# Attention and two MoE layers on one core: values' products of two tiles together, values' sums later, attention a step further ahead

## The chip, the cores and the metric

One core of a Trainium2 chip runs the whole program. The metric is the device time in microseconds (us). The engines are TensorE (PE in the profile, with its weight loads as PEld), VectorE (DVE), ScalarE (ACT), GpSimd (POOL) and SyncE (SP), which here only issues DMAs. Each takes its own instructions in their written order and waits at semaphores for the others.

## The reference

Three layers follow one another. The attention has 4 batches, 8 heads, 576 positions and 64 columns a head; a cumulated bias and a causal mask are added to the scores. Its output is laid out as 2304 tokens of 512 columns. Two feed-forward layers (called MoE) of 2048 inner columns follow, one with a squared ReLU, one with h cos h.

```python
scores = scale * np.matmul(q, k.transpose(0, 1, 3, 2))
cum = np.cumsum(np.maximum(s, 0.0), axis=-1)
bias = -(cum[:, :, :, None] - cum[:, :, None, :])
scores = np.where(causal, -1000000000.0, scores + np.minimum(bias, 0.0))
attn = softmax(scores)                 # with 1e-09 added to the sum
x = np.matmul(attn, v)                 # to 2304 x 512
h = np.maximum(x @ w_in, 0.0);  x = h * h @ w_out
h = x @ w_in2;                  out = (h * np.cos(h)) @ w_out2
```

## The kernel before

The 2304 tokens are cut into nine blocks of 256. Attention produces a block's tokens as a *unit*: eight heads, and in each head tiles of up to 128 queries (128 or 64). There are 160 such tiles, called jobs and numbered in order; the first 32 (heads below `EARLY`, 256 positions) take a short path in f32, the other 128 the path that this text is about. The first MoE layer then works block by block in 16 *chunks* of 128 inner columns: `g1` (line 844, 12 products of 256 columns), then two chunks later `g2` (line 873, 12 products). Every operand is split into a high and a low part, so each product comes three times. The second layer (lines 1230 and 1285) follows from about 620 us on.

Attention is laid between the chunks by hand. `step()` advances the job number i by one and emits, in this order: `g1` or `g2` of one chunk, the evacuation of finished heads on DVE (`evacuate`, ending at line 630), the mask and row minimum of job i-1 (line 510) and the split of job i-2 into two f16 parts `p` (lines 555 and 559) with its transposing DMA on SP (line 565, `p` to `pt`), the low part `gl` of earlier chunks (line 863), the scores of job i on PE (line 496), further chunks, the exponentials on ACT, then the products with the values on PE (`emit_pv`, line 590: 9 to 15 products for a wide tile, 3 or 6 for a narrow one), and the transposes of evacuated heads on PE (`turn`, line 644). `LAG` says how many steps after its scores a job's products with the values come: 3 for the early jobs, 5 for the others. `unit_done` says at which step block u's chunks begin: the lag of its last job and 3 more.

At the end of a block's chunks the two halves of its result leave PSUM: `yst` is copied on ACT (first half) and on DVE (second half), line 881, stored by SP, and squared and summed on ACT (line 884). The next block's first `g2` reuses the same PSUM.

The values themselves are split beside all this: `v_load`, `v_square` (ACT, line 390), `v_sum` (a tiny product on PE over the squares' sums, line 398), `v_scale`, `v_high`, `v_low`, `v_store`. `V_TIME` is the number of steps that `v_steps` reserves for it, `v_add` puts each on its step.

Buffers that matter: `p` has two of 1280 columns, and a third under the tag `p3` for every third job once the first layer's weights are split; `pt` has three; `stg` has two of 2 KB a partition, for weights under way and for `yst`; `pvs`, in which the products with the values gather, has two halves for successive pairs of heads. A tile that finds its pool full is written only when the last user of the buffer it gets has finished.

Of the kernel before, what the change touches and what calls it, by code (L numbers as in the profile page):

```python
# [10 lines left out]
F16 = mybir.dt.float16  # L11
# [12 lines left out]
NF = DFF // 128  # L24
# [9 lines left out]
LAG = (3, 5)  # L34
# [62 lines left out]
EARLY = 16  # L97
# [10 lines left out]
XST_TO = 20  # L108
V_STRIDE = 11
V_NEAR = 6  # L110
V_TIME = 7


@with_exitstack
def attention_moe_moe_kernel(
# [24 lines left out]
    wp = ctx.enter_context(tc.tile_pool(name="wp", bufs=1))  # L140
# [4 lines left out]
    at = at_stack.enter_context(tc.tile_pool(name="at", bufs=1, side="right"))  # L145
# [48 lines left out]
    for x in range(H // 2):  # L194
        t = wp.tile([128, 2, 2 * BT], F32, tag=f"w{2 * NF - (2, 3, 4, 6)[x]}", name="early")
# [113 lines left out]
    for x in range((XST + 1) // 2):  # L309
        t = wp.tile([128, 2, 512], F32, tag=f"w{2 * NF - 5 - x}", name="xst")  # L310
# [6 lines left out]
    jobs = []  # L317
    last_job = {}
# [8 lines left out]
    jd = {}  # L327
    xb = {}
    evq, xtq, xcq = [], [], []
    lag1, wrest = [], []  # L330
# [117 lines left out]
    def v_steps(gs, start):  # L448

        at, due = [], len(jobs) + V_TIME  # L450
        for b, h, n, nch in reversed(gs):
            first = next(
                i for i, j in enumerate(jobs) if j[0] >= 2 * H and heads[j[0]][1] == b and h <= heads[j[0]][2] < h + n
            )
            due = min(first - start + 3 - V_TIME, due - V_NEAR)
            at.insert(0, due)
# [6 lines left out]
    def v_add(gs, at, stored=True):  # L463

        for g, t in zip(gs, at):
            fs = []
            if g not in vs:
                fs, t = [(t, v_load)], t + 2
            fs += [(t, v_square), (t + 1, v_sum), (t + 2, v_scale), (t + 2, v_high), (t + 3, v_low)]
            for x, f in fs + [(t + 3, v_store)] * stored:  # L470
                vq.extend([] for _ in range(x + 1 - len(vq)))
                vq[x].append((f, g))

# [42 lines left out]
        j["sb"], j["nb"] = sb, nb[0:r, len(j["ps"]) - 1:len(j["ps"])]  # L516

    def p_tile(i):
        third = nw[2] >= 2 * NF and not wrest and i % 3 == 2
        return at.tile([128, 1280], F16, tag="p3" if third else "p", bufs=1 if third else 2, name="p")  # L520

    def emit_exp(i):
# [17 lines left out]
    def emit_split(i):  # L540
        n, ti, q, r = jobs[i]
        j = jd[i]
        w, sb = j["w"], j["sb"]
        cw = 128 * ((w + 127) // 128)
        if n < EARLY:
            pp = j["ps"][0][0][:, BT:BT + cw]
            pt = at.tile([128, 640], F32, tag="pt", bufs=3, name="pt1")
            (nc.scalar.copy if ti else nc.vector.tensor_copy)(pt[:, 0:w], pp)
            j["pt"] = pt
            yield  # L550
            return
        p = p_tile(i)
        if cw > w:
            nc.gpsimd.memset(p[0:r, 0:2 * cw].rearrange("p (a c) -> p a c", a=2)[:, :, w:cw], 0.0)
        nc.vector.tensor_scalar(
            out=p[0:r, 0:w], in0=sb[0:r, 0:w], scalar1=PSC, scalar2=None, op0=ALU.mult
        )
        yield
        nc.vector.scalar_tensor_tensor(  # L559
            out=p[0:r, cw:cw + w], in0=sb[0:r, 0:w], scalar=PSC, in1=p[0:r, 0:w],  # L560
            op0=ALU.mult, op1=ALU.subtract,
        )
        pt = at.tile([128, 1280], F16, tag="pt", bufs=3, name="pt")
        pt = pt[:, 0:2 * cw // 128 * r].rearrange("p (a r) -> p a r", r=r)
        nc.sync.dma_start_transpose(out=pt, in_=p[0:r, 0:2 * cw])
        j["pt"] = pt
        yield
# [106 lines left out]
    def job(i):  # L674
        return jobs[i] if 0 <= i < NJ else None

    def lag(i):
        return LAG[not job(i) or jobs[i][0] >= EARLY]

    def heads_ahead(i, *fs):  # L680
        if job(i) and jobs[i][1] == 0:
# [1 line left out]
                upto(cnt, jobs[i][0] + d, f)  # L683

    def unit_done(u):
        return last_job[u] + lag(last_job[u]) + 3


    nw = [2, 0, 0]
    stq = [(wp, 3)]  # L690
    p3 = [0]
# [285 lines left out]
    def softmax_tail(i):  # L977
        if job(i - 1):
            yield from emit_mask(i - 1)
        for j in stage(2, i - 2):  # L980
            yield from emit_split(j)

    def step(moe=0, bits=0, attn=True):
# [37 lines left out]
        if attn:  # L1021
            for j in stage(0, i - 2):
                if jobs[j][1] == 0:
                    load_v(jobs[j][0])
            for j in stage(3, i - LAG[0]):
                if j > i - lag(j):
                    stages[3] -= 1
                    break
                emit_pv(j)
# [104 lines left out]
    while prog[0] < unit_done(0):  # L1134
        i = prog[0]
        x = i - FIRST_BITS
        step(bits=int((x + 1) * PROLOG_BITS) - int(x * PROLOG_BITS) if x >= 0 else 0)

    for k in range(NB1):
        start = prog[0]  # L1140
        goal = unit_done(k + 1) if k + 1 < NB1 else start
        if k == 0:
            gs = [(b, h, 2, 5) for b in V_ORDER for h in range(0, H, 2)]
            v_add(gs, v_steps(gs, start))
# [164 lines left out]
    for i in range(len(steps2) + G2LAG):  # L1309
# [6 lines left out]
        if new:  # L1316
            p, j, f = steps2[i]
# [89 lines left out]
```

## Time and profile before

| | |
|---|---|
| median of 3 runs | 1003.15 us (1000.76 to 1003.25) |
| the profiled execution | 1003.76 us, of which 1002.0 us are its span |
| PE busy | 966.9 us (96%) |
| DVE busy | 723.9 us (72%) |
| ACT busy | 655.5 us (65%) |
| POOL busy | 163.2 us (16%) |
| mean granted clock of PE | 0.995 |

Attention's late jobs lie between about 107 and 560 us. In the rows below, a row of the timeline gives the start in us, the duration in us, engine, line, operation and tiles; xN says that N like instructions in a row are merged into it; a bracket at its end says how long the engine sat idle before it and for what. Successive matmuls overlap, so what a product costs PE is the distance from its start to the next start.

### The profile page before, as it was taken

What the parts mean: (1) busy time and instruction counts of PE and PEld (TensorE: products, weight loads), DVE (VectorE), ACT (ScalarE), POOL (GpSimd) and SP (SyncE); (2) the same over time, 40 slices, a digit from 0 to 9 for tenths busy, and PEclk for the clock granted to TensorE, in tenths of its full rate; (3) what the DMA queues carried; (4) which work ended last, traced back from release to release, by engine and by line L of the source; (5) the groups of instructions that cost most, each with busy time, mean ns of one, the idle gap of its engine ahead of it and who ended that gap; (6) DMA issues with size and microseconds to landing.
All of it is one profiled execution on the core that took longest, in us unless ns stands there. A gap on an engine that the chain in (4) does not pass through costs nothing.

```text
span 1002.0 us, 20487 instructions
## 1 busy us (share of the span) xinstructions
PE 966.9 (96%) x7266; PEld 740.6 (74%) x7266; DVE 723.9 (72%) x1865; ACT 655.5 (65%) x1596; POOL 163.2 (16%) x258
## 2 busy tenths in 40 slices
PE   5999899999999999999999999999999999999998
PEld 4788898899999998999999997444544454444444
DVE  6879788867777897787888267798887545555555
ACT  4789777767777777767776578777766444433433
POOL 2000011111111121111211023330033341000000
PEclk9999999999999999999999999999999999999999
DMA  8955599746887986467898569210000000011001
GB/s 268 292 182 181 118 202 203 170 111 157 196 162 160 178 193 175 109 155 145 192 206 180 188 237 360 95 43 1 1 1 1 0 1 1 0 43 43 23 20 64
DMA packets 150711, 126.65 MB, mean 126 GB/s; under 512 B 108048, under 2 KB 125792, under 8 KB 150608
## 3 DMA queue, kind: packets, MB, share of 16 engines
q1 hardware_dynamic: 146688, 119.05, 46.1%
q0 software_dynamic: 3904, 6.29, 2.5%
q8 instruction: 57, 0.93, 0.4%
q14 instruction: 46, 0.38, 0.1%
q10 hardware_dynamic: 16, 0.01, 0.0%
HBM read 85.25 MB, written 15.81 MB: 101 GB/s over the span
## 4 chain that ended last, share of the span: by engine, by line
PE 79%; DVE 8%; DMA 6%; ACT 4%; issue 2%; SPq 1%; DVEq 0%; ACTq 0%
PE hps L844 18%; PE y L873 18%; PE o L1285 17%; PE hp L1230 17%; PE qkp L496 4%; PE pvs L590 4%; DMA rw<-in_w_dram 3%; DMA raw<-in_qk_dram 1%; PE xps L644 1%; DVE st L716 1%; DVE sb L510 1%; DVE gl L863 1%; DVE wt L737 0%; DVE k L357 0%; SPq L178 0%
## 5 line engine op out<-in xcount | busy, mean ns | idle before, releaser
L844 PE MATMUL hps<-xh,wt 128*128 128x256 f32 x1152 | 241.4, 292 | 4.1 <-ACT g L855 4.0
L873 PE MATMUL y<-gh,wt 128*128 128x256 f32 x1152 | 237.7, 289 | 0.0
L844 PEld LDWEIGHTS hps<-xh,wt 128*128 128x128 f32 x1152 | 191.7, 194 | 7.0 <-ACT g L855 5.5
L873 PEld LDWEIGHTS y<-gh,wt 128*128 128x128 f32 x1152 | 189.9, 192 | 1.3
L1230 PE MATMUL hp<-yh,wt 128*128 128x512 f16 (+1 forms) x640 | 185.9, 358 | 0.0
L1285 PE MATMUL o<-wt,gh 128*128 128x512 f16 x576 | 171.3, 379 | 2.0 <-ACT wt L1300 1.9
L873 PE MATMUL y<-gl,wt 128*128 128x256 f32 x576 | 163.4, 284 | 2.6 <-DVE gl L863 2.6
L844 PE MATMUL hps<-xl,wt 128*128 128x256 f32 x576 | 164.3, 285 | 0.9 <-DVE xl L661 0.9
L1230 PEld LDWEIGHTS <-wt 128*128 128x128 f16 x960 | 92.2, 98 | 93.3
L1242 ACT ACTIVATE a<-hp,hsc 128x512 f32<-128x512 f32 (+1 forms) x80 | 51.4, 643 | 118.6 <-PE hp L1230 117.2
L855 ACT ACTIVATE g<-hps 128x256 f32<-128x256 f32 x144 | 54.6, 379 | 107.7 <-PE hps L844 105.8
L1230 PE MATMUL hp<-yl,wt 128*128 128x512 f16 (+1 forms) x320 | 114.4, 358 | 0.0
L873 PEld LDWEIGHTS y<-gl,wt 128*128 128x128 f32 x576 | 110.6, 192 | 3.7 <-DVE gl L863 3.1
L844 PEld LDWEIGHTS hps<-xl,wt 128*128 128x128 f32 x576 | 111.7, 194 | 1.4 <-DVE xl L661 1.1
L1285 PE MATMUL o<-wt,gl 128*128 128x512 f16 x288 | 109.2, 379 | 0.4 <-DVE gl L1272 0.4
L1243 DVE TENSOR_SCALAR kf<-a 128x512 f32<-128x512 f32 (+1 forms) x80 | 34.5, 431 | 103.8 <-ACT a L1242 103.4
L1285 PEld LDWEIGHTS <-gh 128*128 128x128 f16 x576 | 56.2, 98 | 66.7 <-issue 2.4
L527 ACT ACTIVATE sb<-sb,nb 128x128 f32<-128x128 f32 (+8 forms) x160 | 93.7, 586 | 12.1 <-DVE nb L510 12.0
L339 POOL DMA_DIRECT2D k<-ext_d x80 | 40.8, 510 | 341.9 <-ACT g L856 92.3
L510 DVE CUSTOM_DVE_ANT_0 sb<-qkp,mask 128x128 f32<-128x128 f32 (+8 forms) x160 | 72.7, 454 | 13.8 <-PE qkp L487 8.6
L1251 ACT ACTIVATE a<-kf 128x512 f32<-128x512 f32 (+1 forms) x80 | 46.8, 585 | 46.6 <-DVE kf L1244 46.1
L559 DVE SCALAR_TENSOR_TENSOR p<-sb,p 128x512 f16<-128x512 f32 (+7 forms) x128 | 72.4, 565 | 4.0
(119 smaller groups left out, 1680.1 us busy)
## 6 DMA issues: line engine op xcount, KB each, us to landing
rw<-in_w_dram SPq DMA_DIRECT2D x64, 512.0 KB
raw<-in_qk_dram SPq DMA_DIRECT2D x32, 352.0 KB
raw<-in_qk_dram SPq DMA_DIRECT2D x16, 384.0 KB
v_d<-vt SPq DMA_DIRECT2D x16, 320.0 KB
raw<-in_qk_dram SPq DMA_DIRECT2D x16, 320.0 KB
vb<-v_d SPq DMA_DIRECT2D x32, 160.0 KB
vr<-in_v_dram POOLq DMA_DIRECT2D x15, 320.0 KB, 4.7
y_d<-yst SPq DMA_DIRECT2D x18, 256.0 KB
```

The source lines that it names most:

```text
L339: nc.gpsimd.dma_start(out=hd[n][1][64:68, BT - nq:BT + nl], in_=ext_d[n, :, BT - nq:BT + nl])
L496: nc.tensor.matmul(p[0:r, 0:cn], m[0:kk, qo:qo + r], m[0:kk, BT + c0:BT + c0 + cn], start=(kk == 128), stop=(kk == 68),)
L510: nc.vector.tensor_tensor_reduce(out=sb[0:r, c0:c0 + cn], in0=p[0:r, 0:cn], in1=mask[0:r, mo + c0:mo + c0 + cn], scale=-0.125, scalar=(3.0 ...
L527: nc.scalar.activation(out=sb[0:r, 0:w], in_=sb[0:r, 0:w], func=ACTF.Exp, scale=-1.0, bias=j["nb"], accum_out=pd[n - h % 2]["z"][0:r, ti, ...
L559: nc.vector.scalar_tensor_tensor(out=p[0:r, cw:cw + w], in0=sb[0:r, 0:w], scalar=PSC, in1=p[0:r, 0:w], op0=ALU.mult, op1=ALU.subtract,)
L844: nc.tensor.matmul(hp, w[:, a, c * 128:(c + 1) * 128], (xh, xl)[e][:, c, :], start=(n == 0), stop=(n == 3 * KD - 1),)
L855: nc.scalar.activation(out=g, in_=hp, func=ACTF.Relu)
L873: nc.tensor.matmul(yps[k][d // 2][:, d % 2, :], w[:, a, d * 128:(d + 1) * 128], (gh, gl)[e], start=(f == 0 and n == 0 and d % 2 == 0), sto ...
L1230: nc.tensor.matmul(hp, w[:, a, c * 128:(c + 1) * 128], (yh, yl)[e][:, c, :], start=(m == 0), stop=(m == 3 * KD - 1),)
L1242: nc.scalar.activation(out=a, in_=hp, func=ACTF.Copy, scale=sm["hsc"][:, j, f:f + 1], bias=0.25)
L1251: nc.scalar.activation(out=a, in_=kf, func=ACTF.Sin, scale=-6.2831850)
L1285: nc.tensor.matmul(ops[j][a], (gh, gl)[e][:, a * 128:(a + 1) * 128], w[:, x, :], start=(first and m == 0), stop=(last and m == 2),)
```

## The change

Six edits. The lag of a late job becomes 5 for an even and 4 for an odd number, so that jobs i and i+1 have their products with the values in the same step. `unit_done` adds 4 instead of 3 from the second unit on. The values' sum, scales, high and low parts and store come one step later behind the squares, and `V_TIME` reserves 8 steps. The third `p` buffer serves only jobs of up to 512 positions. Of `pt`, jobs whose number leaves 3 by 4 take other memory: the `p3` buffer where the tile is wider than 512 positions, one of the two `stg` buffers otherwise. The arithmetic is the same.

```diff
-V_TIME = 7
+V_TIME = 8
...
-            fs += [(t, v_square), (t + 1, v_sum), (t + 2, v_scale), (t + 2, v_high), (t + 3, v_low)]
-            for x, f in fs + [(t + 3, v_store)] * stored:
+            fs += [(t, v_square), (t + 2, v_sum), (t + 3, v_scale), (t + 3, v_high), (t + 4, v_low)]
+            for x, f in fs + [(t + 4, v_store)] * stored:
...
-        third = nw[2] >= 2 * NF and not wrest and i % 3 == 2
+        third = nw[2] >= 2 * NF and not wrest and i % 3 == 2 and jd[i]["w"] <= 512
...
-        pt = at.tile([128, 1280], F16, tag="pt", bufs=3, name="pt")
+        if i % 4 < 3:
+            pt = at.tile([128, 1280], F16, tag="pt", bufs=3, name="pt")
+        elif cw > 512:
+            pt = at.tile([128, 1280], F16, tag="p3", bufs=1, name="pt3")
+        else:
+            pt = wp.tile([128, 1024], F16, tag="stg", bufs=2, name="pt4")
...
-        return LAG[not job(i) or jobs[i][0] >= EARLY]
+        if job(i) and jobs[i][0] < EARLY:
+            return LAG[0]
+        return LAG[1] - (i % 2 if job(i) else 0)
...
-        return last_job[u] + lag(last_job[u]) + 3
+        return last_job[u] + lag(last_job[u]) + (4 if u else 3)
```

Line numbers in the changed kernel are higher by 5 (values' products 595, turns 649) or 7 (chunks 851 and 880, copies of `yst` 888).

On PE, before, in the second half of the fourth unit: a wide tile's products with the values (`pvs` from `pt`), two turns (`xps` from `xp`), a values' sum, then a chunk, and the narrow tile of the same head a chunk later.

```order
L844 MATMUL hps_77<-xh_1815,wt_695 128x256
L590 LDWEIGHTS pt_3126
L590 MATMUL pvs_78<-vb_3154,pt_3126 128x64
...
L644 MATMUL xps_79<-ident_85,xp_3259 128x128
L644 MATMUL xps_79<-ident_85,xp_3259 128x64
L398 MATMUL xps_79<-ss_3241,ones_87 128x2
L873 MATMUL y0_2909<-gh_3149,wt_539 128x256
...
L496 MATMUL qkp_3337<-k2_3197 128x256
L590 LDWEIGHTS pt_3185
L590 MATMUL pvs_78<-vb_3154,pt_3185 64x64
```

On PE, after, at the same place: the two tiles of the head stand together.

```order
L851 MATMUL hps_77<-xh_1749,wt_695 128x256
L595 LDWEIGHTS pt_3135
L595 MATMUL pvs_78<-vb_3162,pt_3135 128x64
...
L595 LDWEIGHTS pt_3185
L595 MATMUL pvs_78<-vb_3162,pt_3185 64x64
...
L398 MATMUL xps_79<-ss_3202,ones_87 128x2
L880 MATMUL y0_2932<-gh_3157,wt_539 128x256
```

Over the program the 128 groups of products with the values become 64, all of two tiles: 40 pairs of two 128-row tiles, 8 of two 64-row tiles, 16 of one of each. Of the 48 places with turns, 36 stand right behind such a group before, and none after, because `turn` now falls in the steps between.

On DVE, before, at the end of the first block's chunks (`y1` is the second half of the block's result; the names in brackets are the semaphores that the instruction waits for, DMAHW being DMAs):

```order
L404 TENSOR_SCALAR vsc_89<-xps_79 128x2 [waits PE_49]
L555 TENSOR_SCALAR p_1540<-sb_1466 128x512 [waits Activation_49]
L409 TENSOR_SCALAR vsc_89<-vsc_89 128x2 [waits DVE_49]
L559 SCALAR_TENSOR_TENSOR p_1540<-sb_1466,p_1540 128x512 [waits DVE_49]
L881 COPY yst_1571<-y1_646 128x512 [waits PE_49]
L510 ISA sb_1607,nb_1608<-qkp_1551,mask_86 128x512 [waits DVE_49]
```

On DVE, after, at the same place:

```order
L559 SCALAR_TENSOR_TENSOR p_1583<-sb_1490,p_1583 128x384 [waits DVE_49]
L354 TENSOR_TENSOR hi_1563<-raw_1363,hi_1563 64x256 [waits DMAHW4_49,Activation_49]
L357 TENSOR_TENSOR k2_1564<-raw_1363,hi_1563 64x512 [waits DMASW5_49]
L888 COPY yst_1615<-y1_646 128x512 [waits DMAHW5_49,PE_49,Activation_49]
L425 SCALAR_TENSOR_TENSOR vt_1418<-vr_1314,vsc_89,vt_1418 128x5x64 [waits DMAHW1_49,DMASW4_49]
```

Here one `stg` buffer holds job 35's `pt`, so both halves of `yst` get the other one: the copy of `y1` waits for the store and the squaring of the first half. At the eight later block ends both `stg` buffers are free again.

On DVE, before, in the fourth unit, where its narrow heads begin (job 56's `p`, in the third `p` buffer):

```order
L510 ISA sb_2890,nb_2891<-qkp_2850,mask_86 64x192 [waits DVE_49,PE_49]
L510 ISA nb_2891 64x1
L555 TENSOR_SCALAR p_2893<-sb_2839 128x128 [waits DMAHW3_49,Activation_49,Pool_49]
L559 SCALAR_TENSOR_TENSOR p_2893<-sb_2839,p_2893 128x128 [waits DVE_49]
L661 TENSOR_TENSOR xl_2673<-xps_79,xh_2672 128x64 [waits Activation_49]
```

On DVE, after, the same job:

```order
L510 ISA sb_2914,nb_2915<-qkp_2853,mask_86 64x192
L510 ISA nb_2915 64x1
L555 TENSOR_SCALAR p_2917<-sb_2841 128x128 [waits DMAHW4_49,PE_49,Activation_49]
L559 SCALAR_TENSOR_TENSOR p_2917<-sb_2841,p_2917 128x128 [waits DVE_49]
L354 TENSOR_TENSOR hi_2893<-raw_2766,hi_2893 64x192 [waits DMAHW6_49,Activation_49]
```

Its buffer last held job 55's `pt`, so it now waits for PE: for job 55's products with the values, which stand a step later than this write. The same happens once more, at job 113 behind job 111.

## Rows read from the trace of the kernel before

**Rows 1.** Busy time by stretch: us and instructions of each engine, clock, DMA share, GB/s
```profile
105.00:117.50 12.50, 9.94 (x77) 9.24 (x76) 11.27 (x30) 9.51 (x25) 1.29 (x2) 1.00 0.75 169
...
300.00:350.00 50.00, 50.00 (x496) 48.68 (x495) 39.21 (x104) 38.33 (x103) 6.10 (x11) 1.00 0.83 170
...
505.00:520.00 15.00, 15.00 (x157) 14.83 (x156) 13.71 (x41) 12.13 (x31) 2.15 (x6) 1.00 0.81 191
```

**Rows 2.** Timeline of PE: waits in the attention stretch
```profile
109.97 0.44 PE L644 MATMUL xps<-ident,xp 128*128 128x128 f32 x2 [0.38 <-DVE xp L630]
...
114.25 0.39 PE L844 MATMUL hps<-xl,wt 128*128 128x256 f32 x1 [0.88 <-DVE xl L661]
...
117.74 0.38 PE L398 MATMUL xps<-ss,ones 128*128 128x2 f32 x2 [1.55 <-ACT vt L390]
...
195.55 0.63 PE L590 MATMUL pvs<-vb,pt 128*64 128x64 f16 x15 [1.39 <-DVE xp L630]
...
387.27 0.63 PE L590 MATMUL pvs<-vb,pt 128*64 128x64 f16 x15 [1.11 <-DVE xp L630]
...
523.34 0.39 PE L844 MATMUL hps<-xh,wt 128*128 128x256 f32 x1 [1.40 <-ACT g L855]
```

**Rows 3.** Busy time by stretch, right behind two of these waits
```profile
117.50:122.50 5.00, 4.76 (x25) 4.57 (x26) 1.22 (x4) 1.50 (x6) 0.37 (x1) 0.66 0.17 58
...
195.00:200.00 5.00, 4.45 (x34) 4.34 (x34) 4.03 (x16) 3.08 (x10) 0.55 (x2) 0.66 1.38 311
```

**Rows 4.** Timeline of PE: a wide tile's nine products between two chunks
```profile
301.78 0.28 PE L844 MATMUL hps<-xh,wt 128*128 128x256 f32 x1
301.90 0.43 PE L590 MATMUL pvs<-vb,pt 128*128 128x64 f16 x9
302.17 0.36 PE L873 MATMUL y<-gh,wt 128*128 128x256 f32 x1
302.38 0.28 PE L873 MATMUL y<-gl,wt 128*128 128x256 f32 x1
```

**Rows 5.** Timeline of PE: a 64-row tile's fifteen products behind the scores
```profile
396.23 0.28 PE L496 MATMUL qkp<-k 68*128 68x256 f32 x1
396.44 0.66 PE L590 MATMUL pvs<-vb,pt 128*64 128x64 f16 x15
...
397.25 0.28 PE L844 MATMUL hps<-xl,wt 128*128 128x256 f32 x1
```

**Rows 6.** Timeline of PE: a turn alone, and a turn behind fifteen products
```profile
505.88 0.33 PE L644 MATMUL xps<-ident,xp 128*128 128x128 f32 x1
...
506.17 0.28 PE L844 MATMUL hps<-xl,wt 128*128 128x256 f32 x1
...
517.34 0.61 PE L590 MATMUL pvs<-vb,pt 128*128 128x64 f16 x15
...
518.05 0.28 PE L844 MATMUL hps<-xl,wt 128*128 128x256 f32 x1
```

**Rows 7.** Waits of SP's queue: us in total, times, longest
```profile
SPq L565 <- PE pvs L590: 81.5, 71, 3.9
```

**Rows 8.** Timeline: the two copies at the end of the first block
```profile
122.39 0.59 ACT L881 COPY yst<-y 128x512 f32<-128x512 f32 x1 [0.31 <-PE y L873]
...
123.11 0.69 DVE L881 COPY yst<-y 128x512 f32<-128x512 f32 x1 [3.72 <-PE y L873]
```

**Rows 9.** DMA issues of the page: KB each, median us from issue to landing
```profile
vr<-in_v_dram POOLq DMA_DIRECT2D x15, 320.0 KB, 4.7
...
k<-ext_d POOLq DMA_DIRECT2D x32, 11.0 KB, 3.3
```

**Rows 10.** Timeline of the last unit: writes of p, one transposing DMA, its landing
```profile
529.18 0.46 DVE L555 TENSOR_SCALAR p<-sb 128x576 f16<-128x576 f32 x1
...
531.67 1.32 SPq L565 DMA_TRANSPOSE pt<-p  x1
...
535.16 0.20 POOL L554 MEMSET p<- 128x128 f16 x1 [0.23 <-DMA pt<-p]
...
537.24 0.46 DVE L555 TENSOR_SCALAR p<-sb 128x576 f16<-128x576 f32 x1
```

## The prediction

> **What bounds the kernel now.** I read the busy times first, by engine and then by stretch. PE is at 96% of the span, and in the middle of the attention it has no gap at all: 50.00 of 50 us, while DVE has 39 and ACT 38 [rows 1]. There a microsecond less on PE is a microsecond less of the program, and nothing else helps. In the stretch before it, while the first layer's weights are still being split, DVE is the tight one (11.27 of 12.5 us, PE 9.94), and in the last unit both are (13.71 and 15.00 of 15) [rows 1]. Then I went along PE's timeline for its waits. Six matter here [rows 2]: at 109.97 a turn and at 114.25 the first chunk of the second block wait for DVE, which is just finishing the unit before; at 117.74 the values' sum waits 1.55 for squares that ACT made a step earlier; at 195.55 and 387.27 the products with the values wait 1.39 and 1.11 for DVE to empty the accumulator, both times right after a block's end, where DVE also had a copy to do; at 523.34 a chunk waits 1.40 for ACT, which stood waiting for a load. Behind two of them the granted clock is 0.66 over 5 us [rows 3]: part of that stretch at the lower of the two levels, 1.7 us of clock lost each (0.34 x 5). Last I looked at what PE pays between two chunks.
>
> **The switch between kinds of products.** Consecutive products of a chunk start 0.12 apart (301.78 to 301.90). From 301.78 to 302.38, two such starts, it is 0.60; nine products with the values took 0.27 of it (301.90 to 302.17, 0.03 each), so 0.60 - 0.24 - 0.27 = 0.09 is the price of leaving the chunk and coming back, paid in the first product behind (0.21 in place of 0.12) [rows 4]. For a 64-row tile it is more: 396.23 to 397.25 is 1.02; less 0.24, and less 15 products at about 0.033 (0.66 less one product's 0.19 latency, over 14 steps; estimate) makes 0.28 [rows 5]. With 128 groups made into 64, 40 pairs save 0.09 each (3.6), 8 pairs of 64-row tiles 0.28 each (2.3), and 16 mixed pairs 0.09 each if the narrow half still pays all of its 0.28 (1.4): 7.3 us together. What a mixed join costs no row shows: between nothing (then it saves up to 0.28 a pair) and a whole narrow switch more, 7.3 lies between about 3 and 10; I take the middle one, since the narrow switch is measured.
>
> Against that stand the turns. Behind a group they ride on its switch: 517.34 to 518.05 is 0.71, less 0.45 for 15 products, 0.12 for one chunk product due and 0.09 for the switch, so a single turn costs 0.05. Alone, with its start 0.12 behind the product before it, 0.12 + 0.29 - 0.24 = 0.17 [rows 6]. So each of the 36 places that lose their group costs 0.12 more, 4.3 us. The values' sums (16) lose theirs about half the time, under 1 us, and I leave them in the range. **First term: -7.3 + 4.3 = -3.0 us** (-6 to +1).
>
> The Trainium skill (TensorE: Matmul & The Clock Gate, "Step-by-step: what each phase is for") speaks against this term: the next tile's weights are loaded while the present tile's matmul runs, so a change of tile should cost no time. Inside one kind of product the trace agrees (0.12 each, with loads beside them). At the change of kind it does not, and by rows 4 the first product behind is 0.09 late. By the page the term would be 0 and the whole sum 3.0 higher; the measurement decides.
>
> **Values' sums later, attention ahead.** The sum's wait at 117.74 goes, because a full step lies between squares and sum. With the unit finished one step before its block begins, the waits at 109.97 and 114.25 go too. Together 0.38 + 0.88 + 1.55 = 2.8 us, and with the clock behind the last one (1.7) 4.5. But DVE is at nine tenths there [rows 1] and all the work remains, with one attention step more put ahead of the second block; part of what PE no longer waits for here it waits for a little later. **Second term: -2.5 us** (-4.5 to +1).
>
> **Accumulator emptied in time.** A pair of heads' last products and the next pair's first were a step apart, with DVE's emptying of `pvs` between. Now two steps lie between, as products come every second step only. The waits of 1.39 and 1.11 go, with 1.7 of clock at most: 4.2. At both places DVE is late for what follows as well (its copies of `yst` have just been made), so I take half. **Third term: -2.0 us** (-4.2 to 0).
>
> **SP's queue.** With three `pt` buffers each transposing DMA waited for the products with the values of three jobs earlier: 81.5 us over 71 waits [rows 7], and loads of raw heads stood behind it on SP. With a fourth place for `pt` this wait is gone. Almost all of it hid; where it showed is 523.34, ACT waiting for such a load. I take half of those 1.40. **Fourth term: -0.7 us** (-2.8 to 0).
>
> **The copy of y1.** At the first block's end DVE's copy now waits for the store of the other half, and ACT's squaring of it waits for DVE. From the moment `y0` is complete: 0.59 for ACT's copy [rows 8], a store of 256 KB that no row shows, bounded by the page's loads at 3.3 (11 KB) and 4.7 (320 KB) [rows 9], 0.69 for DVE's copy: 4.6 to 6.0. In that time PE has the other half of the chunk, a chunk, the scores and half of the next block's first `g2`: 24 products of 0.12 and two long ones at about 0.24 (twice a 256-column product, estimate), 3.3. Left over: 1.3 to 2.7; with lost clock up to 4.4; nothing if PE is late there anyway; a gain is excluded, as nothing is taken away. **Fifth term: +2.0 us** (0 to +4.4).
>
> The Trainium skill (DMA: Bandwidth & Descriptors, "Anatomy of one DMA") puts a DMA at about 2.0 us fixed, most of it the receipt of a write, and bytes over 436e3; that is an estimate of 2.6 us for this store. By it the copy would be ready after 3.9 us, PE would wait 0.6, and the sum would be 1.4 lower. No row here shows a store's landing.
>
> **Edits that I cost at nothing.** At jobs 56 and 113 DVE waits at the write of `p` for PE. What is queued behind it on DVE is the next head's low parts and the next chunks' `gl`; PE has one chunk (1.4 us) ahead of the next scores and about four us of work ahead of the `gl` concerned, and DVE has room there. Uncovered it would be about 1 us each, inside the range. Two `p` buffers where a tile is wider than 512: the transposing DMA landed at 535.16, 6.0 after its write of `p` began at 529.18, and the next but one write begins at 537.24 [rows 10], so 2.1 us are left, and SP's wait inside the 6.0 goes. The step that the unit is ahead changes no count: late units had lag 5 + 3 behind an odd last job, and have 4 + 4.
>
> **Sum.** -3.0 - 2.5 - 2.0 - 0.7 + 2.0 = -6.2 us against the profiled execution's 1003.76 us: 997.6. The execution lay 0.6 above the median of the runs shown; I forecast 997.5 us, 0.56% below it. What a measurement of this kernel can tell from no change is about 0.3%, 3 us: faster is below 1000.1, slower above 1006.2.
>
> **Rivals.**
> *DVE takes it back.* The waits removed were all on DVE or ACT, and these have as much to do as before. If PE only meets them at the next place, terms two to four come to nothing and the copy of `y1` stays: 1003.8 - 3.0 + 2.0 = 1002.8. For it: DVE at 90% around 110 us and in the last unit. Against it: from 300 to 350 it is at 78%, and DVE itself waited 3.72 for PE at 123.11 [rows 8]. No change.
> *All of it stays.* Terms two to four in full and the copy hidden: 1003.8 - 3.0 - 4.5 - 4.2 - 2.8 = 989.3.
> *Two p buffers bind (slower).* In the last unit and in the first halves of the fourth and the seventh, 32 steps, a write of `p` may have to wait for the transposing DMA of two jobs earlier. It decides from a landing 2.1 us later than in rows 10; 0.8 us beyond that costs 0.4 a step, 32 x 0.4 = 12.8 less what the other terms gain (6.2): 1010. For it: the queues are full there and the buffer that goes was used. Against it: the DMA now starts earlier.
> *No switch saved.* By the page's rule the first term is 0, and with the others 1000.6: no change.
>
> **How the numbers follow.** The forecast has a chance of 0.47 (its own range 993 to 1000), all of it stays 0.14, DVE takes it back 0.25, two p buffers 0.10, no switch saved 0.04. Of the forecast's share nearly all is faster: 0.47 + 0.14 = 0.61. Within 0.3%: 0.25 + 0.04 = 0.29. Slower: 0.10. The range of 8 in 10 leaves out the slower rival and half of the largest gain: 990.5 to 1004.0.
>
> **What would show it.** Products with the values on PE in 64 groups, each switch still 0.09 or 0.28, turns alone at 0.17; no wait at the values' sums and none of PE for DVE's emptying behind a block's end; SP's wait for products with the values nearly gone; one wait of PE of one to three us at the first `g2` of the second block, with DVE and ACT idle before it. The prediction is wrong if busy PE between 200 and 500 us does not get shorter by about 2 us, if PE's waits between 100 and 200 us add up to as much as before, or if DVE waits for transposing DMAs in the wide units.

## The result, and the profile after

Forecast: 997.5 us. Measured: 1007.92 us, the median of 8 runs (1004.71 to 1011.15), against 1001.68 us for the kernel before in the same runs (1000.62 to 1003.25). The ratio is 1.0058, interval 1.0039 to 1.0078: slower by about 6 us, outside the range (990.5 to 1004.0). The profiled execution took 1007.96 us. The profiled execution of before, on which the sum was made, lay with 1003.76 us above all eight of these runs.

The page after, span and busy times:

```profile
span 1006.2 us, 20471 instructions
PE 964.5 (96%) x7266; PEld 741.5 (74%) x7266; DVE 721.1 (72%) x1865; ACT 654.6 (65%) x1596; POOL 162.6 (16%) x258
```

PE is busy for 2.4 us less than before, and the span is 4.2 us longer. The stretches after, first two disturbed ones and then an undisturbed one (columns as in [rows 1]):

```profile
80.00:100.00 20.00, 16.67 (x112) 16.10 (x111) 16.10 (x43) 16.34 (x44) 1.06 (x3) 0.83 0.60 206
205.00:215.00 10.00, 6.89 (x57) 6.35 (x58) 7.06 (x31) 4.02 (x12) 0.52 (x2) 0.83 0.31 79
276.48:350.83 74.35, 74.35 (x751) 73.06 (x749) 56.19 (x155) 56.67 (x153) 8.47 (x19) 1.00 0.84 172
```

The same stretches in the kernel before, the first and the third of these:

```profile
80.00:100.00 20.00, 17.73 (x145) 17.13 (x144) 18.26 (x48) 18.96 (x50) 0.73 (x1) 1.00 0.60 205
270.01:344.95 74.94, 74.94 (x755) 73.21 (x751) 56.62 (x154) 56.23 (x154) 8.53 (x19) 1.00 0.85 168
```

In the undisturbed stretch, the same five quarters of a block's work in both, PE is full and the change is 0.59 us faster. From 80 to 100 us all three engines do less than before, and the granted clock is 0.83: 3.4 us of clock gone in 20. The loss comes in the first 270 us: there the third block's chunks end, 6.9 us later than before (ACT has made its copy of `yst` at 269.34, before at 262.47), and from there to the end the distance shrinks to 4 us. These are the waits of the early part and one later wait for `pt`; rows of several engines of the kernel after, in order of time:

```profile
88.61 0.47 ACT L390 ACTIVATE vt<-vr 128x320 f16<-128x320 f32 x1 [2.07 <-DMA v_d<-vt]
...
91.21 0.69 DVE L744 TENSOR_TENSOR wt<-st,wt 128x512 fp32r<-128x512 f32 x1 [2.80 <-ACT wt L732]
...
91.73 0.44 PE L538 MATMUL qkp<-ident,sb 128*128 128x128 f32 x2 [1.56 <-ACT sb L527]
...
125.20 3.17 SPq L889 DMA_DIRECT2D y_d<-yst  x2
...
127.33 0.69 DVE L888 COPY yst<-y 128x512 f32<-128x512 f32 x1 [2.94 <-DMA y_d<-yst]
...
128.08 0.39 PE L880 MATMUL y<-gh,wt 128*128 128x256 f32 x1 [1.35 <-DVE yst L888]
...
136.67 0.52 PE L595 MATMUL pvs<-vb,pt 128*128 128x64 f16 x12 [0.74 <-DMA pt<-p]
...
170.86 0.74 POOL L379 DMA_DIRECT2D vr<-in_v_dram  x1 [7.17 <-ACT gh L864]
...
176.94 0.32 PE L496 MATMUL qkp<-k 68*64 68x288 f32 x1 [2.41 <-DMA k<-ext_d]
...
205.67 0.63 PE L595 MATMUL pvs<-vb,pt 128*64 128x64 f16 x15 [0.77 <-DMA vb<-v_d]
...
206.40 0.23 DVE L555 TENSOR_SCALAR p<-sb 128x128 f16<-128x128 f32 x1 [4.90 <-PE pvs L595]
...
208.74 0.38 PE L398 MATMUL xps<-ss,ones 128*128 128x2 f32 x2 [2.44 <-DVE xl L666]
...
247.77 0.38 PE L595 MATMUL pvs<-vb,pt 128*64 128x64 f16 x6 [1.29 <-DMA pt<-p]
...
405.39 0.38 PE L595 MATMUL pvs<-vb,pt 128*64 128x64 f16 x6 [0.79 <-DMA pt<-p]
```

Four things are to be seen. ACT's squares of the next values wait for the store of the last ones out of the same `vt`; behind them on ACT stand a copy of weights, for which DVE waits, and an exponential, for which PE waits. The copy of `y1` waits for the store, and PE for the copy, as forecast. GpSimd stands 7.2 us before a load of values, and the loads of `k` (from `ext_d`) queued behind it reach PE 2.4 us late. Job 56's `p` stops DVE for 4.9 us; `xl`, which must be read out of the PSUM tile that the values' sum writes, is queued behind it on DVE, and PE waits 2.4 us. In the kernel before, the same load of values, and PE's wait for the same exponential:

```profile
168.41 0.75 POOL L379 DMA_DIRECT2D vr<-in_v_dram  x1 [2.86 <-PE qkp L496]
```

```profile
89.67 0.44 PE L538 MATMUL qkp<-ident,sb 128*128 128x128 f32 x2 [0.56 <-ACT sb L527]
```

SP's waits, summed, against [rows 7]. Where SP waited for the products with the values, it now waits for `p` itself, the DMA's own input:

```profile
SPq L570 <- DVE p L559: 125.7, 91, 4.0
...
SPq L570 <- PE pvs L595: 5.8, 5, 1.9
```

The first of these in the kernel before:

```profile
SPq L565 <- DVE p L559: 45.8, 49, 3.6
```

The switches of the kernel after: a pair of 64-row tiles between two chunks, a pair of 128-row tiles, and two turns alone:

```profile
192.50 0.28 PE L880 MATMUL y<-gh,wt 128*128 128x256 f32 x1
192.71 1.14 PE L595 MATMUL pvs<-vb,pt 128*64 128x64 f16 x30
193.78 0.39 PE L851 MATMUL hps<-xh,wt 128*128 128x256 f32 x1
194.00 0.28 PE L851 MATMUL hps<-xl,wt 128*128 128x256 f32 x1
...
307.92 0.28 PE L851 MATMUL hps<-xh,wt 128*128 128x256 f32 x1
308.04 0.79 PE L595 MATMUL pvs<-vb,pt 128*128 128x64 f16 x21
308.66 0.36 PE L880 MATMUL y<-gh,wt 128*128 128x256 f32 x1
308.87 0.28 PE L880 MATMUL y<-gl,wt 128*128 128x256 f32 x1
...
311.85 0.29 PE L851 MATMUL hps<-xh,wt 128*128 128x256 f32 x1
311.97 0.38 PE L649 MATMUL xps<-ident,xp 128*128 128x128 f32 x2
312.11 0.36 PE L880 MATMUL y<-gh,wt 128*128 128x256 f32 x1
312.31 0.28 PE L880 MATMUL y<-gl,wt 128*128 128x256 f32 x1
```

From 307.92 to 308.87 are 0.95; less 0.24 for two starts and 0.62 for 21 products (0.0295 each) that leaves 0.09, the price of one switch, now paid once for two tiles. From 192.50 to 194.00 are 1.50; less 0.24 and 0.99 (30 products at 0.033) that leaves 0.27, again once. From 311.85 to 312.31 are 0.46; less 0.24, the two turns cost 0.22: by the forecast's prices 0.17 for the first and 0.05 for the second.

### The profile page after: what moved, and what is told of

It is laid out like the page before. It is cut to its first block, busy times and chain, and to the rows that moved or that the text cites. A ratio compares the mean times of both kernels' runs of the same rounds, so it can differ in the third digit from the quotient of the medians.

```text
span 1006.2 us, 20471 instructions
## 1 busy us (share of the span) xinstructions
PE 964.5 (96%) x7266; PEld 741.5 (74%) x7266; DVE 721.1 (72%) x1865; ACT 654.6 (65%) x1596; POOL 162.6 (16%) x258
## 4 chain that ended last, share of the span: by engine, by line
PE 44%; DVE 3%; ACT 2%; issue 1%; DVEq 0%; ACTq 0%
PE o L1292 17%; PE hp L1237 17%; PE y L880 5%; PE hps L851 5%; PE qkp L496 1%; PE pvs L595 1%; ACT wt L738 0%; DVE kf L1251 0%; DVE wt L747 0%; DVE a L1264 0%; DVE wsc L777 0%; DVE kf L1250 0%; ACT a L1249 0%; ACT a L1258 0%; ACT gh L1272 0%
## 5 line engine op out<-in xcount | busy, mean ns | idle before, releaser
L870 DVE TENSOR_TENSOR gl<-g,gh 128x256 fp32r<-128x256 f32 x144 | 61.1, 425 | 24.6 <-PE y L880 15.4
```

What stands on the lines that cost most here:

```text
L870: nc.vector.tensor_tensor(out=gl, in0=g, in1=gh, op=ALU.subtract)
```

## The experiments

Each ratio is to the kernel before in the same runs, with its 95% interval; 0.1% is 1 us. A difference between two of the ratios is uncertain by some 2 to 3 us either way. V stands for the values' part, P for the pairs, U for the attention step ahead of the second block, M for the buffers; the change is P, U, M and V.

### One part put back

**Values put back (P, U, M).**

```diff
...
-            fs += [(t, v_square), (t + 2, v_sum), (t + 3, v_scale), (t + 3, v_high), (t + 4, v_low)]
+            fs += [(t, v_square), (t + 1, v_sum), (t + 2, v_scale), (t + 2, v_high), (t + 3, v_low)]
...
```

The store goes back with them, and `V_TIME` to 7.

> The changed kernel with the values' part put back (sum one step behind the squares, store three, 7 steps reserved); pairs, buffers and the unit ahead stay. Theory: the later store is what costs 5 us between 80 and 111 us (ACT's squares wait 2.07 us at 88.61 for the store of the values before, PE then waits 1.77 and 1.56 us and has 3.4 us of lower clock). Here that goes, and the sum's wait of 1.5 us with 1.7 us of clock around 118 comes back: 1006 us, 2 below the changed kernel. Rival: the later sums are the gain and something else costs: the time rises by 3 us, to 1011.

Measured 1.0038 (1.0022 to 1.0053): 2 us won back, as the theory's sum said, but not by its parts. The sum's wait at 118 us did not return: the step ahead alone removes it.

**Buffers put back (P, U, V).**

```diff
...
-        if i % 4 < 3:
-            pt = at.tile([128, 1280], F16, tag="pt", bufs=3, name="pt")
...
+        pt = at.tile([128, 1280], F16, tag="pt", bufs=3, name="pt")
```

> The changed kernel with the buffers put back (third p for all widths, three pt); pairs, values and the unit ahead stay. Theory: the write of p of job 56 no longer waits for the products of job 55 (4.9 us on DVE at 206 us, 2.4 us on PE and 1.7 us of clock behind it), and the copy of y1 no longer for the store (1.35 us on PE at 128): 5 us less than the changed kernel, 1003. Rival: with three pt the transposing DMA waits for the pair's products again and lands later, and PE's waits for pt (3.3 us now) grow: 1008 or more.

The third `p` buffer serves all widths again. 1.0038 (1.0022 to 1.0054): 2 us, not 5. DVE no longer waits at job 56 and PE not for the copy of `y1`; PE's waits for `pt` were 2.5 us, against 3.3 in the changed kernel.

**The step ahead put back (P, M, V).**

```diff
-        return last_job[u] + lag(last_job[u]) + (4 if u else 3)
+        return last_job[u] + lag(last_job[u]) + (4 if u > 1 else 3)
```

> The changed kernel with only the attention step ahead of the second block put back (17 steps beside the first block, not 18). Theory: the step is moved, not saved; the start of the second block is 3 us earlier and the first block's later part 3 us longer, with PE's waits at 110 and 114 us (1.3 us) back: within 1.5 us of the changed kernel, 1007.9. Rival: DVE is the bound beside the first block, and a step more there costs its 3 us for good: 1005.

1.0097 (1.0074 to 1.0120): both were wrong, the step ahead is worth some 4 us here. Its waits at 110 and 114 us came back, and PE waited 2.88 us at 90 us and 3.6 for `k` at 176.

**Values and the step ahead alone (U, V).** The two edits in the kernel before.

> The kernel before with the values' part and the attention step ahead alone; no pairs, buffers as before. Theory: the later store costs 5 us before 111 us, the waits at 110, 114 and 118 us with their clock (4.5 us) go: 1002 us, no change against before. Rival: the later store costs nothing without the other edits, and the gain of 4.5 us stays: 997.

1.0073 (1.0048 to 1.0097): 7 us slower with no pairs and the old buffers. Neither theory; the loss is in V or U. The runs spread from 1002.2 to 1013.6 us, and the profiled one took 1003.4: its trace can show at most 3 of these 7 us.

### One part alone

**Values alone (V).**

> The kernel before with the values' part alone (sum, scales, parts and store a step later, 8 steps reserved). Theory: the values' buffers are held a step longer while the next group comes after the same 11 steps, so ACT's squares wait for the store (2 us each, twice or more) and GpSimd's load of the next values waits 7.2 us in place of 2.9, with the loads of k queued behind it (PE waits 2.5 us around 172 us): 3 us or more slower than before, 1004. Rival: what the earlier run with values and unit ahead lost (0.73%) came from the unit ahead: within 1 us of before.

1.0054 (1.0034 to 1.0074): as the theory has it. Here U brings nothing on top (1.0073 with it). PE's wait at 90 us, against the 0.56 of before:

```profile
91.44 0.69 PE L538 MATMUL qkp<-ident,sb 128*128 128x128 f32 x2 [3.13 <-ACT sb L527]
```

A wait of PE of 1.4 to 3.1 us at about 91 us stands in the traces of all nine kernels with the whole values' part, and in no trace without it (at most 0.57 there).

**Pairs alone (P).**

> The kernel before with the pairs alone (lag 5 for even and 4 for odd jobs); values, buffers and the unit ahead as before. Theory: pairs save 3 us of switches net (block starts at 264 to 567 us drew 2.6 us nearer in the changed kernel) and lose about as much again in PE's waits for pt of the odd job, which has one step less for its transposing DMA (2.5 us in 2 waits in the run with old buffers): within 1 us of before. Rival: the pairs cost nothing, 997.5; or pairs are the loss, 1003 or more.

0.9998 (0.9983 to 1.0013): no change, with PE waiting 3.0 us for `pt` in 4 places and 1.4 for `vb`. This trace also holds the wait for the squares of [rows 2] once more, and the 5 us behind it:

```profile
116.77 0.38 PE L398 MATMUL xps<-ss,ones 128*128 128x2 f32 x2 [1.55 <-ACT vt L390]
```

```profile
117.00:122.00 5.00, 5.00 (x57) 4.87 (x57) 2.52 (x7) 3.02 (x8) 0.51 (x1) 1.00 0.11 40
```

The clock is 1.00 where it was 0.66 behind the same wait before [rows 3].

**Pairs and the step ahead (P, U).**

> The kernel before with pairs and the attention step ahead of the second block; values and buffers as before. Theory: values and buffers carry the loss (2 us each in the changed kernel), pairs and the step ahead are worth nothing to -3 us: 998 to 1001, no slower than before. Rival: the step ahead costs for itself in the stretch beside the first block, where DVE is at nine tenths: 1003.

0.9974 (0.9960 to 0.9989): faster. P and U together are a gain, if a small one; V and M carry the loss.

### What in the values' part costs

Groups of values follow each other by 6 steps. The low parts came 5 steps behind a group's load and come 6 behind it now: on the step of the next load into the same `vr`. It is the front of the chain that moved: with `V_TIME` at 8 every group but the first begins a step earlier, so that its load and squares come earlier (the second group's squares at 88.61, at 91.25 before) while its sum, parts and store keep their step.

**The low parts and the store on their old step.**

```diff
-            fs += [(t, v_square), (t + 1, v_sum), (t + 2, v_scale), (t + 2, v_high), (t + 3, v_low)]
+            fs += [(t, v_square), (t + 2, v_sum), (t + 3, v_scale), (t + 3, v_high), (t + 3, v_low)]
```

> The kernel before with the values' sum and scales a step later and the high parts too, but the low parts and the store on their old step, and 7 steps reserved as before. Theory: the loss of 0.54% of the values' part comes from low parts and store moving onto the very step of the next group's load (groups are 6 steps apart, the load came 1 step behind the low parts and comes beside them now); with these two on their old step the load of values on GpSimd waits 3 us again, k is in time, and the time is within 2 us of before. Rival: the later sum itself is the loss: 1004 to 1005 as with the whole part.

1.0059 (1.0038 to 1.0081). The run does not decide: PE's long wait at 90 us and its wait for `k` were gone, and ACT's for the store, but the edit brought a wait of its own, low parts right behind the high parts on the same step:

```profile
DVE vt L425 <- ACT vt L418: 21.8, 16, 2.3
```

**The load a step later too.**

```diff
-                fs, t = [(t, v_load)], t + 2
+                fs, t = [(t + 1, v_load)], t + 2
```

> The kernel before with the whole values' part a step later, and the load of each group's values a step later too, so that it again comes a step behind the low parts of the group before. Theory: GpSimd's wait of 7.2 us shrinks to 3 and PE's wait for k (2.5 us) goes; what the store's landing costs ACT stays, and the squares may wait for the load itself: about half of the 0.54% is won back, 1002.5. Rival: the loads are not the matter and the store is: 1004 to 1005.

V with the load back on its old step: 1.0011 (0.9994 to 1.0028), 4 us better than V alone. GpSimd's wait at the same load, V alone and then with the later load:

```profile
167.86 0.73 POOL L379 DMA_DIRECT2D vr<-in_v_dram  x1 [6.76 <-ACT sb L527]
```

```profile
167.57 0.75 POOL L379 DMA_DIRECT2D vr<-in_v_dram  x1 [2.86 <-PE qkp L496]
```

PE's wait for `k` (2.0 us in V alone) is gone with it. The wait of ACT for the store stays, and PE's behind it (2.80 us at 91.20).

**The same in the changed kernel.** The same edit, nothing else.

> The changed kernel with the load of each group's values one step later, nothing else. Theory: in the changed kernel too most of the values' loss is the load standing on GpSimd's queue before the low parts that free its buffer: 0.58% above before becomes 0.2 to 0.3%. Rival: beside the pairs the store and the longer chain are the loss: 0.5% or more stay.

1.0057 (1.0036 to 1.0079): the rival. The wait for `k` is gone from the profile, and this profiled execution is 4.6 us ahead of the changed kernel's at 392 us, past job 56's wait. It loses 3.4 of that at job 113: the products at 402.60 wait 1.81 us for `pt` (0.79 in the changed kernel, at 405.39), and the granted clock is 0.84 and 0.81 in the two stretches of 5 us from 400 (1.00 in the changed kernel). Why the time shows nothing won is not settled by one execution.

### What the buffers cost

**Jobs 56 and 113 without their wait.**

```diff
-        third = nw[2] >= 2 * NF and not wrest and i % 3 == 2 and jd[i]["w"] <= 512
+        third = nw[2] >= 2 * NF and not wrest and i % 3 == 2 and jd[i]["w"] <= 512 and i not in (56, 113)
```

> The changed kernel with p of jobs 56 and 113 in one of the two ordinary p buffers, so that they no longer wait for the products of jobs 55 and 111; all else stays. Theory: DVE's wait of 4.9 us at 206 us goes, with PE's 2.4 us at the values' sum behind it and 1.7 us of clock: 3 to 4 us less than the changed kernel, 1004. Rival: PE meets the wait elsewhere (its own at the products of the pair, 205.67, or the sum itself): within 1 us of the changed kernel.

1.0028 (1.0012 to 1.0044): 3 us less than the changed kernel, as expected. The step with job 56's wait, from one `g1` to the next on PE, takes 6.0 us in this trace and 10.1 in the changed kernel's.

**All three waits of M away, V put back.** The last run with the values' part of before, and job 35's `pt` in an ordinary place.

```diff
-        if i % 4 < 3:
+        if i % 4 < 3 or i == 35:
```

> The changed kernel with the values' part put back, p of jobs 56 and 113 in ordinary buffers, and job 35's pt in an ordinary one (so that the copy of y1 has its own buffer): pairs, the step ahead, and the extra place for pt without its three waits. Theory: the extra place is then worth SP's 81 us of waits, which cost little: equal to pairs and step ahead within 1.5 us, 0.26% under before. Rival: the wide tiles' two p buffers cost by themselves: no better than before.

0.9954 (0.9937 to 0.9970), 996.11 us: under both kernels. Its clock and PE's largest waits from 100 to 600 us:

```profile
core 0: 995.1 us, clock 1.000
```

```profile
PE qkp L496 <- DVE nb L510: 2.2, 5, 0.6
PE pvs L595 <- DMA pt<-p: 2.0, 3, 1.2
PE pvs L595 <- DMA vb<-v_d: 1.6, 2, 1.1
```

**The wait of the copy of `y1` back.** Job 35's `pt` again beside `yst`.

> Pairs, the step ahead and the extra place for pt, values as before, p of jobs 56 and 113 in ordinary buffers; the copy of y1 again waits for the store of the other half (it did not in the run that was 0.46% under before). Theory: this wait costs its 1.35 us on PE and the clock behind it, 2 to 3 us: 0.2% under before. Rival 1: it costs 5 us, as what jobs 56 and 113 leave of the distance between 0.38% above and 0.46% under before: no better than before. Rival 2: PE is late there anyway: 0.46% under before.

0.9972 (0.9959 to 0.9986). The copy costs some 2 us, not clear of noise (the two intervals overlap): PE waits 1.36 us at 124.69, and the 5 us from 124 have a granted clock of 0.76, the 5 behind them 0.90. The 5 us of rival 1 are elsewhere. This run differs from the first of all (values put back) only by jobs 56 and 113, and by 6.6 us; job 56's step takes 9.9 us there and 6.3 here. The place in that first run, DVE and PE and the stretch behind:

```profile
202.52 0.23 DVE L555 TENSOR_SCALAR p<-sb 128x128 f16<-128x128 f32 x1 [4.75 <-PE pvs L595]
...
204.86 0.38 PE L398 MATMUL xps<-ss,ones 128*128 128x2 f32 x2 [2.44 <-DVE xl L666]
```

```profile
205.00:210.00 5.00, 5.00 (x28) 4.66 (x29) 3.75 (x19) 2.02 (x7) 0.20 (x1) 0.66 0.42 101
```

And job 56 in the run without it, where it waits for its buffer's own DMA:

```profile
197.38 0.23 DVE L555 TENSOR_SCALAR p<-sb 128x128 f16<-128x128 f32 x1 [0.97 <-DMA pt<-p]
```

**All of the change, with the three waits of M away and the load of values later.**

> The whole change with four repairs: p of jobs 56 and 113 and job 35's pt in ordinary buffers, and each group's values loaded a step later; the values' part stays. Theory: the later load takes away the values' loss, and the sum's wait at 118 us (1.5 us and 1.7 us of clock) is gone as well: equal to or under the run without the values' part, 0.46 to 0.6% under before. Rival: the store a step later still costs ACT and PE some 2 us between 80 and 100 us: 0.2 to 0.3% under before.

0.9985 (0.9971 to 0.9998): the rival. V still costs 3 us against the run without it. The wait that is left of V is the one for the store, ACT's row and PE's from 80 to 100 us here (without V the first of PE's waits is the same, and the second is not there):

```profile
ACT vt L390 <- DMA v_d<-vt: 3.7, 2, 2.0
```

```profile
83.60 0.33 PE L538 MATMUL qkp<-ident,sb 128*128 128x128 f32 x1 [1.76 <-ACT sb L527]
...
90.45 0.44 PE L538 MATMUL qkp<-ident,sb 128*128 128x128 f32 x2 [3.05 <-ACT sb L527]
```

That this wait is the 3 us is argued, not shown: the execution profiled here was the fastest of its twelve (997.11 us), within 0.2 us of the one profiled without V (996.92). A second `vt` buffer, which would set the store apart, was not run.

### Pairs one step later

```diff
-        return LAG[1] - (i % 2 if job(i) else 0)
+        return LAG[1] + 1 - (i % 2 if job(i) else 0)
```

> Pairs and the attention step ahead, with the pairs' products one step later (lag 6 for even and 5 for odd jobs); values and buffers as before. Theory: the odd job's transposing DMA has its old five steps again, so PE's waits for pt (2 to 3 us) go while the switches stay saved: 2 us less than pairs and step ahead alone (which gave 0.26% under before), so 0.45% under before. Rival: the even job's pt is held a step longer, SP's queue stands behind it and raw heads come late: no better than 0.26% under before.

The lags are 6 and 5, and the blocks begin on the same steps as with the pairs. 1.0301 (1.0274 to 1.0329). Both halves came true, and the second is 30 us. PE's wait for `pt` is nearly gone; SP stands behind three `pt` that are held a step longer, and the raw heads queued behind are late for ACT:

```profile
PE pvs L590 <- DMA pt<-p: 0.2, 1, 0.2
```

```profile
SPq L565 <- PE pvs L590: 160.3, 54, 8.1
```

```profile
ACT hi L346 <- DMA raw<-in_qk_dram: 53.1, 21, 6.2
```

## Why the prediction was wrong

The runs give a sequence from the best version to the change, one edit at a time: 0.9954, with the wait of `y1` 0.9972, with the values' part 1.0028, with jobs 56 and 113 1.0058. In us: -4.6, then +1.8, +5.6 and +3.0.

**First term, switches (-3.0): right on PE, and not won alone.** 64 groups, and each switch 0.09 or 0.27 as before. In the undisturbed stretch 10 groups were saved and 5 places of turns stood alone: by the forecast's prices -0.9 and +0.6, measured -0.59 in all, a little better than forecast. What it left out is the other side: the odd job of a pair has one step less between `p` and its products, and PE waited 3.3 us for `pt` in 4 places, where it had not waited before. With the pairs came this term and the third, -5.0 by the forecast; alone, with the old buffers, they gave nothing (0.9998). Their trace gives the balance: the waits for `xp` of 2.5 us are gone, and 3.0 for `pt` and 1.4 for `vb` have come.

**Second term, values' sums later and attention ahead (-2.5): failed.** It put two edits under one gain. The step ahead is the gain: the waits of [rows 2] at 114.25 and 117.74 go by it alone (that at 109.97 grew, from 0.38 to 1.3 us with P and U alone), and it is worth 2.4 us beside the pairs (0.9998 to 0.9974) and some 4 in the changed kernel; without the pairs no gain of it shows. The longer chain of the values bought nothing and cost 5.4 us alone, 5.6 in the sequence above. The step of the prediction that failed: it followed the sum and its wait, and not the two buffers that the values' chain holds a step longer. `vt` is squared into again while its store is on the way (ACT 2.07 us, in the stretch where DVE and ACT are nearly full, and with it PE and the clock). `vr` is loaded on the very step on which it comes free, and GpSimd's queue stands before that load with the `k` of the next heads behind it. The later load, in the trace and in the time, shows the second in the kernel before, 4 us; in the changed kernel the trace shows it and the time does not. Of the first the traces show the wait, in every kernel with the whole part; its price, the 3 us that remain with all repairs, is argued.

**The clock in the second and third terms.** Both counted 1.7 us of lost clock behind a wait, read from one execution that lay above all runs of the result. With the pairs alone the same wait for the squares left the clock at 1.00, and with the values alone so did the wait for `xp` (1.43 us at 196.10, 1.00 from 196 to 201). The loss does not follow every such wait, and a gain from removing it was not to be counted in full.

**Third term, accumulator emptied in time (-2.0): the waits went, the gain did not show.** PE no longer waits for `xp` at the values' products behind a block's end, but at the same two places for `vb` (1.3 us together).

**Fourth term, SP's queue (-0.7): right in kind.** 81.5 us over 71 waits became 5.8 over 5, and ACT's late load at 523.34 is gone. What the extra place is worth between 0.9974 and 0.9954 the intervals do not settle.

**Fifth term, the copy of `y1` (+2.0): right, the size partly by luck.** PE waited 1.35 us, the runs give 1.8 with lost clock, not clear of noise. The store took 2.1 us from its issue at 125.20 to the copy at 127.33, less than the lower bound from loads (3.3). That the wait still came out at the low end of the forecast is luck: ACT, busy with other work, began its copy of `y0` at 124.60, 1.3 us after the last product of `y0` ended, which the sum had not. The Trainium skill (DMA: Bandwidth & Descriptors, "Anatomy of one DMA") gives its 2.0 us and bytes over 436e3 for a DMA issued by GpSimd, and this store is issued by SP; its estimate of 2.6 us was all the same nearer than the loads.

**Edits costed at nothing: failed at jobs 56 and 113.** The waits on DVE were 4.9 and 2.6 us, not about 1. The prediction named what is queued behind on DVE as the next head's parts and `gl`, and had room for them; it missed `xl` and with it the values' sum on PE, 2.44 us and the clock behind it. The price is 3.0 us in the changed kernel and 6.6 without V. The two are each uncertain by over 2 us, so that they differ is hardly shown; in the traces job 56's step is shorter by 4.0 us in the one and 3.6 in the other.

**The slower rival, two `p` buffers in the wide units: not what happened.** DVE waited at the write of `p` once for a transposing DMA, 1.9 us in the last unit, and the best version (0.9954) has the same two `p` buffers in these units.

**The sign that was named.** PE's waits between 100 and 200 us add up to 6.7 us, against 7.3 before: hardly less, so that the forecast's own test came out at its edge. PE's busy time fell by 2.4 us over the program, as the first term has it.

## What to carry to other kernels

A chain stretched by a step also holds its buffers longer: for each one, find the next writer and the queue on which that writer waits, and then what stands behind it in that queue. Price a wait by the engine that is stopped (all that follows on it up to the next instruction that PE needs). Do not add lost clock to a gain from one execution alone. Undoing one part at a time gave 2 us for the values' part and 2 for the buffers, each with an uncertainty of its own size; parts put in alone, and a version with all known waits removed, told them apart.

## What was not expected of the hardware

A store of 256 KB freed its buffer 2.1 us after its issue began, while loads of 320 KB and 11 KB have medians of 4.7 and 3.3 us from issue to landing [rows 9]. Of the granted clock: in the run with the values put back, the stretch behind the wait of 2.44 us at 204.86 ran at 0.66 for 5 us, partly on the lower of the two levels. One and the same wait can have either clock behind it: that for the copy of `y1` left 1.00 in the changed kernel (1.35 us, 128 to 133), and 0.76 and then 0.90 in the kernel without V and without the waits of jobs 56 and 113 (1.36 us, 124 to 134); that for the squares 0.66 before and 1.00 with the pairs alone. The best version kept 1.000 with some 10 us of shorter waits between 100 and 600 us.
